# First loads on two queues, roots by GpSimd pow, and a first unit halved along its contraction

## The chip, the cores and the metric

The kernel runs on one core of one Trainium2 chip. The metric is the device time in microseconds (us) of one execution. Engine names are those of the profile: PE is TensorE, DVE is VectorE, ACT is ScalarE, POOL is GpSimd, SP is SyncE. PEld is PE's weight load; a q after a name (SPq) is that engine's sequencer, which issues the loads. In the profile's names xn is normalized x, tp its transpose as PE writes it, sp_ps the output of the warm-up, and bp a product of the Fourier part, which ACT copies to Bs.

## The reference, cut to what matters

```python
def _layernorm(x, axis=-1, eps=1e-5):
    m = jnp.mean(x, axis=axis, keepdims=True); v = jnp.var(x, axis=axis, keepdims=True)
    return (x - m) / jnp.sqrt(v + eps)

def reference(A_x, A_w_r, A_w_i, B_x, B_w_gate, B_w_up, B_w_down):
    # _A_ref: irfft2(rfft2(xn) * (w_r + 1j * w_i)), over 2048 x 512
    # _B_ref: (gelu(xn @ w_gate) * (xn @ w_up)) @ w_down, 512 -> 1792 -> 512
    x = A_x                                   # 1 x 2048 x 512, bf16
    xn = _layernorm(x, axis=-1)
    return x + _A_ref(xn, A_w_r, A_w_i) + _B_ref(xn, B_w_gate, B_w_up, B_w_down)
```

## The kernel before

The rows of x are cut into 16 chunks of 128 rows. Chunks 0 and 1 are loaded singly, normalized, transposed on PE and multiplied at once with the first 512 columns of the gate weights (Wg) and up weights (Wu). PE can do nothing useful before that, so the kernel has it multiply zeros ("spin"), first on zeros alone, then on x chunk 0 (x0), to get its clock up. A small planner in the kernel orders all later work from hand-written estimates of durations and landing times; that order is fixed when the kernel is built.

```python
    pin(nc.scalar.activation(out=root[:], in_=eps_t[:], func=AF.Sqrt, ...))   # loads the Sqrt table
    load_x(0, 1); load_x(1, 1)                       # all on nc.sync
    nc.sync.dma_start(out=idx_t[:], ...)             # a small index table
    load_w(Wg_sb, 0, 512); load_w(Wu_sb, 0, 512)
    load_x(2, 2)
    # ... further loads of weights and x, all on nc.sync
    for k in range(25):                              # warm-up of PE
        pin(nc.tensor.matmul(sp_ps[:, :P if k < 20 else D], lhsT=spin[:],
                             rhs=spin[:] if k < 20 else x_t[:, 0, :], start=True, stop=True))
    def spin_on():                                   # six more, after x0's transposes
        for k in range(6):
            nc.tensor.matmul(sp_ps[:, :256], lhsT=spin[:], rhs=x_t[:, 0, :256], ...)
    # ...
    # 1/sqrt(var + eps): chunks 0, 1 by ACT's Sqrt and DVE's reciprocal;
    # chunks 2, 3 by a bit trick and two Newton steps on DVE (8 instructions),
    # chunks 4 to 15, four at a time, the same way on POOL (10 instructions, then 2 for a bias)
```

## Time and profile before

| | before |
|---|---|
| median time (3 runs; 4 with the rounds of the changed kernel) | 179.47 us (179.32) |
| span of the profiled run | 177.5 us |
| PE busy | 172.1 us, 97% |
| x0 lands, first statistics start | 3.00 us |
| first g_ps (gate product of the first unit) | 6.34 us |
| first u_ps (up product of the first unit) | 7.79 us |
| first y_ps (down phase) | 119.52 us |

The first view is the page's busy table and the chain of work that ended last, as shares of the span, of the kernel before.

```profile
PE 172.1 (97%) x1115; PEld 96.0 (54%) x1133; DVE 116.6 (66%) x261; ACT 96.5 (54%) x171; POOL 20.1 (11%) x60
...
PE 83%; ACT 5%; DMA 3%; issue 3%; POOL 2%; DVE 1%; SPq 1%; ACTq 0%
```

PE is the limit. After the first u_ps it has next to no idle time, so a gain must come from the first 8 us, or from one of the few gaps left. PE's waits name one such gap, 0.4 us. The columns are the waiting instruction, what it waited for, the total, the count and the longest.

```profile
PE bp L581 <- ACT Bs L551: 0.4, 1, 0.4
```

The next view is the timeline of the kernel before: start, duration, engine, line, operation, output and inputs, shape, count; in brackets the idle time before it and what ended that.

```profile
0.80 0.86 SPq L271 DMA_DIRECT2D x_t<-in_A_x_dram  x2
...
2.18 0.43 SPq L275 DMA_DIRECT2D Wg_sb<-in_B_w_gate_dram  x1
2.65 0.51 SPq L275 DMA_DIRECT2D Wu_sb<-in_B_w_up_dram  x1
3.00 0.69 DVE L338 BATCH_NORM_STATS2 stats<-x_t 128x6 f32<-128x512 bf16 x1 [1.99 <-DMA x_t<-in_A_x_dram]
```

The same kernel's PE alone:

```profile
1.05 2.31 PE L318 MATMUL sp_ps<-spin 128*128 128x128 bf16 x20 [1.05 <-DVE eps_t L264]
3.16 2.34 PE L318 MATMUL sp_ps<-x_t,spin 128*128 128x512 bf16 x5
5.29 0.56 PE L350 MATMUL tp<-ident_t,xn 128*128 128x128 bf16 x4
5.69 0.82 PE L323 MATMUL sp_ps<-x_t,spin 128*128 128x256 bf16 x6
6.34 0.61 PE L505 MATMUL g_ps<-xnT,Wg_sb 128*128 128x128 bf16 x8
...
7.04 0.61 PE L505 MATMUL g_ps<-xnT,Wg_sb 128*128 128x128 bf16 x8
7.79 1.07 PE L505 MATMUL u_ps<-xnT,Wu_sb 128*128 128x128 bf16 x16
```

PE starts at 1.05 us and, up to the transposes (tp), never stops. The merged durations overlap, so the pace is to be read from starts. The 20 warm-up matmuls of 128 columns take from 1.05 to 3.16: 106 ns each. The six of 256 columns take from 5.69 to 6.34, again 108 ns each, for twice the columns. Between the two PE's clock doubled. "Half clock" below means the pace of about 107 ns for 128 columns, "full clock" the pace of about 55.

### The profile page before, as it was taken

The numbers are of one execution on the slowest core, as the hardware profiler recorded it, in microseconds if no ns is written. First come the engines' busy times: TensorE is split into PE (matmuls) and PEld (weight loads), VectorE is DVE, ScalarE is ACT, GpSimd is POOL, SyncE is SP. The second block draws the span as 40 slices with busy tenths as digits, with TensorE's granted clock in tenths as the row PEclk, the third lists the DMA queues.
The fourth block names the chain that finished last, engine by engine and source line by source line (L and its number), as shares of the span: only waits on it lengthen the run. The fifth ranks groups of instructions, "written<-read, shape, count | busy, mean of one in ns | idle before, by whom it ended". The sixth has DMA issues, their size and how long they took to land.

```text
span 177.5 us, 3118 instructions
## 1 busy us (share of the span) xinstructions
PE 172.1 (97%) x1115; PEld 96.0 (54%) x1133; DVE 116.6 (66%) x261; ACT 96.5 (54%) x171; POOL 20.1 (11%) x60
## 2 busy tenths in 40 slices
PE   7999999998999999999999999999999999999993
PEld 5798845464455554555555545454445444444463
DVE  3499999873933599998699999543526334344333
ACT  4463286979575989799999955453112111211200
POOL 1000534810676000000000000000000000000000
DMA  3999994243282752121202520200132222221212
GB/s 92 350 382 378 368 180 92 59 98 55 60 291 95 245 173 59 33 55 31 63 6 55 148 60 5 59 0 4 51 97 89 72 78 63 89 85 62 78 44 59
DMA packets 21872, 19.36 MB, mean 109 GB/s; under 512 B 8480, under 2 KB 20000, under 8 KB 21856
## 3 DMA queue, kind: packets, MB, share of 16 engines
q1 hardware_dynamic: 21440, 17.84, 34.6%
q0 software_dynamic: 416, 1.32, 2.5%
q8 instruction: 9, 0.15, 0.3%
q14 instruction: 7, 0.06, 0.1%
HBM read 13.38 MB, written 2.10 MB: 87 GB/s over the span
## 4 chain that ended last, share of the span: by engine, by line
PE 83%; ACT 5%; DMA 3%; issue 3%; POOL 2%; DVE 1%; SPq 1%; ACTq 0%
PE y_ps L820 27%; PE u_ps L505 23%; PE g_ps L505 22%; DMA Wu_sb<-in_B_w_up_dram 3%; PE dp L639 2%; ACT Bs L551 2%; PE yp L772 2%; PE gp L742 2%; PE y_ps L824 2%; PE ep L648 2%; ACT xn L467 2%; ACT ge L510 1%; DVE hT L515 1%; PE bp L581 1%; POOL t L366 0%
## 5 line engine op out<-in xcount | busy, mean ns | idle before, releaser
L505 PE MATMUL u_ps<-xnT,Wu_sb 128*128 128x512 bf16 (+2 forms) x267 | 56.9, 341 | 0.3
L505 PE MATMUL g_ps<-xnT,Wg_sb 128*128 128x512 bf16 (+2 forms) x265 | 56.4, 340 | 0.4
L515 DVE TENSOR_TENSOR hT<-u_ps,ge 128x512 bf16<-128x512 f32 x56 | 38.5, 688 | 19.0 <-PE u_ps L505 10.5
L820 PE MATMUL y_ps<-Wd_sb,hT 128*128 128x512 bf16 (+2 forms) x246 | 50.6, 355 | 0.3
L510 ACT ACTIVATE ge<-g_ps 128x512 bf16<-128x512 f32 x56 | 33.9, 606 | 21.4 <-PE g_ps L505 17.6
L505 PEld LDWEIGHTS <-Wu_sb 128*128 128x128 bf16 x272 | 24.9, 98 | 21.4 <-DMA Wu_sb<-in_B_w_up_dram 0.3
L505 PEld LDWEIGHTS <-Wg_sb 128*128 128x128 bf16 x272 | 24.8, 98 | 20.0
L820 PEld LDWEIGHTS <-hT 128*128 128x128 bf16 x252 | 23.2, 98 | 22.4
L778 ACT CAST yf<-yp 128x512 bf16<-128x512 f32 x16 | 9.3, 586 | 40.5 <-PE yp L772 40.5
L827 DVE TENSOR_TENSOR y_sb<-y_ps,y_sb 128x512 bf16<-128x512 f32 (+2 forms) x18 | 11.1, 631 | 30.0 <-PE y_ps L824 30.0
L653 ACT CAST E<-ep 64x512 bf16<-64x512 f32 x32 | 18.6, 580 | 1.3 <-PE ep L648 0.8
L338 DVE BATCH_NORM_STATS2 stats<-x_t 128x6 f32<-128x512 bf16 x16 | 10.5, 677 | 3.9 <-DMA x_t<-in_A_x_dram 3.9
L467 ACT ACTIVATE xn<-x_t,nb,rstd 128x512 bf16<-128x512 bf16 x12 | 9.7, 827 | 1.8 <-POOL nb L378 1.8
L551 ACT CAST Gs<-gp 128x512 bf16<-128x512 f32 x16 | 8.9, 592 | 0.9 <-PE gp L742 0.9
L551 ACT CAST ds<-dp 128x512 bf16<-128x512 f32 x16 | 9.0, 597 | 0.6 <-PE dp L639 0.5
L551 ACT CAST Bs<-bp 128x512 bf16<-128x512 f32 x16 | 8.4, 607 | 0.5 <-PE bp L581 0.5
L784 DVE TENSOR_TENSOR lv<-yf 128x512 bf16<-128x512 bf16 x16 | 6.1, 422 | 1.5 <-ACT yf L778 0.6
L772 PEld LDWEIGHTS <-Gs 128*128 128x128 bf16 x64 | 4.8, 98 | 3.5
L791 DVE TENSOR_TENSOR yt<-lv 128x512 bf16<-128x512 bf16 x16 | 6.1, 422 | 0.3
L824 PE MATMUL y_ps<-yt,RI_t 128*128 128x512 bf16 (+2 forms) x18 | 6.1, 355 | 0.0
L772 PE MATMUL yp<-CT,Gs 128*128 128x128 bf16 x64 | 6.0, 219 | 0.0
L742 PEld LDWEIGHTS <-F 128*128 128x128 bf16 x64 | 4.5, 98 | 2.6
(72 smaller groups left out, 123.2 us busy)
## 6 DMA issues: line engine op xcount, KB each, us to landing
F<-F SPq DMA_DIRECT2D x32, 64.0 KB, 2.0
y_sb<-in_A_x_dram SPq DMA_DIRECT2D x16, 128.0 KB, 2.1
out_dram<-y_sb SPq DMA_DIRECT2D x15, 128.0 KB, 1.7
x_t<-in_A_x_dram SPq DMA_DIRECT2D x7, 256.0 KB, 8.6
Wd_sb<-in_B_w_down_dram SPq DMA_DIRECT2D x1, 1792.0 KB, 7.5
Wg_sb<-in_B_w_gate_dram SPq DMA_DIRECT2D x2, 512.0 KB, 5.2
Wu_sb<-in_B_w_up_dram SPq DMA_DIRECT2D x2, 512.0 KB, 7.4
Wg_sb<-in_B_w_gate_dram SPq DMA_DIRECT2D x1, 768.0 KB, 10.4
```

The costliest lines, as they stand in the source:

```text
L338: V.bn_stats(out=st[:], in_=x_t[:, c, :])
L467: xn_op[c] = add("ACT", 0.72, lambda c=c: A.activation(out=xn[:, c, :], in_=x_t[:, c, :], func=AF.Identity, bias=nb[:, c:c + 1], scale=rst ...
L505: T_.matmul(b[name][:, f], lhsT=W_[:, e, (f0 + f) * P:(f0 + f + 1) * P], rhs=rhs[:, e, :], start=(e == 0), stop=(e == NE - 1))
L510: A.activation(out=b["ge"][:], in_=b["g_ps"][:], func=AF.Gelu_apprx_tanh)
L515: V.tensor_tensor(out=hT_of(sb, f0, m, o, w), in0=b["u_ps"][:], in1=b["ge"][:], op=ALU.mult)
L551: A.copy(out=o, in_=i)
L653: A.copy(out=b["E"][64 * h:64 * h + 64, r], in_=b["ep", h][64 * r:64 * r + 64])
L772: T_.matmul(t[:, q], lhsT=late["G"][:, q, c0 + j], rhs=IQ[q], start=(q == 0), stop=(q == 3), skip_group_check=True)
L778: A.copy(out=b["yf"][:, j], in_=b[j][:])
L820: T_.matmul(b[o][:], lhsT=hT_of(sb, f, 1, cl * P, P)[:, 0], rhs=Wd_sb[:, f, o:o + w], start=(f == 0), stop=False)
L824: T_.matmul(b[o][:], lhsT=late["RI"][:, c, :], rhs=late["yt"][:, c, o:o + w], start=False, stop=True)
L827: V.tensor_tensor(out=b["y"][:, o:o + w], in0=b[o][:], in1=b["y"][:, o:o + w], op=ALU.add)
```

## The change

Its intent is to start the real matmuls sooner. The first four loads are issued by two sequencers at once. The warm-up on x0 becomes shorter, so that it does not stand before the transposes. The first unit's gate product starts on the first half of the contraction. Roots after the first two chunks take two GpSimd instructions instead of eight on DVE or ten on GpSimd. The planner's figures of landing times are moved to match, and with them the order of later instructions.

```diff
-    pin(nc.scalar.activation(out=root[:], in_=eps_t[:], func=AF.Sqrt, ...))
-    load_x(0, 1)
-    load_x(1, 1)
+    pin(load_x(0, 1))
+    pin(load_x(1, 1, nc.scalar))
+    pin(load_w(Wg_sb, 0, 512))
+    pin(load_w(Wu_sb, 0, 512, nc.scalar))
+    pin(nc.scalar.activation(out=warm[:], in_=eps_t[:], func=AF.Sqrt, ...))
-    nc.sync.dma_start(out=idx_t[:], ...)      # now issued after the loads of x
-    load_w(Wg_sb, 0, 512)
-    load_w(Wu_sb, 0, 512)
     ...
-    for k in range(25):
-        pin(nc.tensor.matmul(sp_ps[:, :P if k < 20 else D], lhsT=spin[:],
-                             rhs=spin[:] if k < 20 else x_t[:, 0, :], ...))
+    for k in range(32):
+        pin(nc.tensor.matmul(sp_ps[:, :P], lhsT=spin[:],
+                             rhs=spin[:] if k < 20 else x_t[:, 0, :P], ...))
     def spin_on():
         for k in range(6):
-            nc.tensor.matmul(sp_ps[:, :256], lhsT=spin[:], rhs=x_t[:, 0, :256], ...)
+            nc.tensor.matmul(sp_ps[:, :P], lhsT=spin[:], rhs=x_t[:, 0, :P], ...)
     ...
-    def rsqrt_steps(U, c0, n): ...             # bit trick and two Newton steps
+    def root_eps(c0, n):                       # y = var + eps; y = pow(y, -0.5)
+        plus_eps(nc.gpsimd, c0, n)
+        nc.gpsimd.tensor_tensor(out=y, in0=y, in1=minus_half[:, 0:n], op=ALU.pow)
     ...
-        g = split("g_ps", "G", Wg_sb, 1000 + k, WG_LAND, 2 if k == 0 else m)
+        if k == 0:                             # e = 0, 1 after the first copy, e = 2, 3 after the second
+            g = add("PE", occ / 2, lambda: mm_half(0), [xT_op[0, 0]], ...)
+            g = add("PE", occ / 2, lambda: mm_half(1), [xT_op[0], g], ...)
     # cut: planner's landing times, chunk 1's copy moved to DVE, the last phase's first group in four pieces
```

## The prediction

> **What bounds the kernel.** TensorE. The busy table has it busy 172.1 of 177.5 us; the chain that ended last is 83% PE. From the first real matmul (g_ps, 6.34 us in the timeline) to the last (174.7) PE hardly stops: the table by stretches leaves about 1.5 us idle, of which the waits name 0.31 us for the second weight tile (Wu lands at 7.74) and 0.45 us at 40.9 (bp, for ACT's copies). So the change can mainly win by starting the real stream earlier. The tail, 2.8 us after the last matmul, is untouched.
>
> **The head now (timeline).** x_t is there at 3.0; statistics 0.69, mean, sqrt on ACT, reciprocal; xn's first half at 4.58, second to 5.26. The first transposes begin at 4.98, the rest only at 5.29, behind five warm-up matmuls of 512 columns (3.16 to about 5.3). Copies end at 6.24. SyncE issues everything: Wg at 2.18 (lands about 6.3), Wu at 2.65 (7.74). After g_ps and four transposes u_ps starts at 7.79; no gap until 40.9.
>
> **What changes.**
> - Wg is issued about 0.95 us and Wu 1.4 us sooner. The Trainium skill, "DMA: Bandwidth & Descriptors", section "Issuing engines are not separate DMA queues", says both issuers run on the same 16 engines and only issue time is saved; the trace fits (Wg, Wu, x2-3 arrive as one stream, 512 KB in 1.44 us, 365 GB/s). I estimate Wg at 5.5 to 6.2 (it now shares with Wu), Wu at 6.5 to 6.9, x2-3 at 7.5 to 8.1.
> - Shorter warm-up lets the transposes start when xn is there, and the first unit starts on half the contraction: g_ps at 5.7 to 6.1. After 16 matmuls (0.94 us) and four transposes (0.23), u_ps at about 6.8: 0.9 to 1.0 us gained.
> - Chunks 2-3: eight DVE steps (1.55 us, 9.98 to 11.53) become two GpSimd steps. Its small steps come every 0.28 us; I take pow for one of these, so 0.6 us with hand-overs. But PE now reaches these transposes at about 10.3 instead of 12.66 (fewer matmuls in front), and VectorE puts one hT product (0.69) before xn. I expect a new PE wait of 0.2 to 0.5 us.
> - Later fours: ten GpSimd steps before the bias become two, 2.2 us less each time, but PE does not wait for that chain: little, perhaps part of the 0.45 us.
> - Last phase's first group cut in four, Wd before RI: nothing.
>
> **On the critical path:** +0.95 (head) -0.3 (chunks 2-3) +0.2 (bp): about 0.9 us.
>
> **Predicted: 178.6 us, range 177.7 to 179.5.** Faster by over 2%: 0.02; within 2%: 0.96; slower: 0.02.
>
> **What would show it.** First g_ps at 5.7 to 6.1, first u_ps near 6.8 with hardly a wait for Wu; first statistics still at 3.0 to 3.2; pow 0.2 to 0.3 us; a PE gap of 0.2 to 0.5 near 10.5 before the transposes; from 45 us on everything about 0.9 us earlier, the down phase at about 118.2 instead of 119.1, at the same pace; same tail.
>
> **What would make it wrong.** (1) The clock: the skill's "TensorE: Matmul & The Clock Gate", Part 1, says PE runs at half rate until a window of some 3.4 us was busy. This trace: 107 to 115 ns per 128 columns until about 5.6, 55 after. The shorter warm-up leaves PE idle between about 4.5 and 5.0; if the full clock comes later, up to 32 matmuls cost 50 ns more each, and the gain is gone. (2) pow slow on GpSimd; over 1 us it stalls PE directly. (3) Wg landing at 6.5, sharing with Wu. (4) x0 sharing with x1, coming later and pushing the whole head.

## The result, and the profile after

The changed kernel takes 180.24 us (median of 4, 180.05 to 180.50), the kernel before 179.32 (median of 4). Executions over 1.5% slower than the fastest of the same kernel are left out of the means. Ratios here are the mean time of one kernel's runs over that of the other's of the same rounds, so they are not quite the ratio of the quoted medians. This one is 1.0054, with a 95% interval of 1.0033 to 1.0074. The change costs 0.9 us; a gain of 0.7 was forecast.

The busy table and the chain of the changed kernel:

```profile
PE 173.5 (97%) x1140; PEld 97.4 (55%) x1140; DVE 116.0 (65%) x255; ACT 95.6 (54%) x170; POOL 17.3 (10%) x38
...
PE 95%; DMA 2%; DVE 1%; issue 0%
```

PE is a little busier, for the same real work (of the 25 further records seven are warm-up, and 18 are matmuls whose records the trace before lacks). Most of that extra time is the half clock, which the timeline shows. Here are the lines that answer to those of before. The ACTq line of x1 is new; Wu is issued by ACTq at 1.23.

```profile
0.80 0.40 ACTq L273 DMA_DIRECT2D x_t<-in_A_x_dram  x1
...
0.80 0.39 SPq L273 DMA_DIRECT2D x_t<-in_A_x_dram  x1
...
1.23 0.46 ACTq L277 DMA_DIRECT2D Wu_sb<-in_B_w_up_dram  x1
1.25 0.42 SPq L277 DMA_DIRECT2D Wg_sb<-in_B_w_gate_dram  x1
...
3.99 0.69 DVE L340 BATCH_NORM_STATS2 stats<-x_t 128x6 f32<-128x512 bf16 x1 [2.97 <-DMA x_t<-in_A_x_dram]
```

PE alone, changed kernel, up to 9.5 us (the last line is cut there; u_ps has 16 matmuls):

```profile
1.05 2.31 PE L320 MATMUL sp_ps<-spin 128*128 128x128 bf16 x20 [1.05 <-DVE minus_half L266]
4.00 1.44 PE L320 MATMUL sp_ps<-x_t,spin 128*128 128x128 bf16 x12 [0.64 <-DMA x_t<-in_A_x_dram]
5.98 0.71 PE L352 MATMUL tp<-ident_t,xn 128*128 128x128 bf16 x4 [0.53 <-DVE xn L346]
6.49 0.85 PE L325 MATMUL sp_ps<-x_t,spin 128*128 128x128 bf16 x6
7.13 1.91 PE L499 MATMUL g_ps<-xnT,Wg_sb 128*128 128x128 bf16 x16
8.83 0.56 PE L352 MATMUL tp<-ident_t,xn 128*128 128x128 bf16 x4
9.23 0.44 PE L491 MATMUL u_ps<-xnT,Wu_sb 128*128 128x128 bf16 x5
```

First, x0's statistics start at 3.99 instead of 3.00, although x0 is still the first load of its queue and is issued at the same 0.80. Second, the 16 gate matmuls take from 7.13 to 8.83, 106 ns each: PE is at half clock all through the first unit's gate product and the transposes after it, until about 9.2. The first u_ps comes 1.44 us later than before. The down phase starts at 120.58 instead of 119.52, 1.06 later, so 0.38 us is won back in between; the wait of bp for ACT is no longer in PE's list. The tail of 2.8 us after the last matmul is unchanged.

The landing times, from the table of DMA issues (KB each, median us from issue to landing), before and then after:

```profile
x_t<-in_A_x_dram SPq DMA_DIRECT2D x2, 128.0 KB, 2.3
```

```profile
Wu_sb<-in_B_w_up_dram ACTq DMA_DIRECT2D x1, 512.0 KB, 6.2
...
x_t<-in_A_x_dram ACTq DMA_DIRECT2D x1, 128.0 KB, 3.4
x_t<-in_A_x_dram SPq DMA_DIRECT2D x1, 128.0 KB, 3.2
```

The two single chunks of x took 2.3 us; now they take 3.2 and 3.4. Wu, issued at 1.23, lands at about 7.4 (1.23 + 6.2) instead of 7.74, so issuing it 1.4 us sooner brought 0.3.

### The profile page after: what moved, and what is told of

The parts are those of the page before. It is cut to its first block, busy times and chain, and to the rows that moved or that the text cites. A ratio compares the mean times of both kernels' runs of the same rounds, so it can differ in the third digit from the quotient of the medians.

```text
span 178.5 us, 3122 instructions
## 1 busy us (share of the span) xinstructions
PE 173.5 (97%) x1140; PEld 97.4 (55%) x1140; DVE 116.0 (65%) x255; ACT 95.6 (54%) x170; POOL 17.3 (10%) x38
## 4 chain that ended last, share of the span: by engine, by line
PE 95%; DMA 2%; DVE 1%; issue 0%
PE u_ps L491 27%; PE y_ps L818 27%; PE g_ps L491 27%; PE gp L739 2%; PE yp L769 2%; PE dp L636 2%; PE bp L578 2%; PE y_ps L822 2%; PE ep L645 2%; DMA x_t<-in_A_x_dram 2%; PE tp L352 1%; PE g_ps L499 1%; DVE stats L340 1%; PE sp_ps L325 0%; DVE xn L346 0%; DVE y_sb L825 0%
## 5 line engine op out<-in xcount | busy, mean ns | idle before, releaser
L491 PEld LDWEIGHTS <-Wg_sb 128*128 128x128 bf16 x256 | 23.9, 98 | 20.6
L453 ACT ACTIVATE xn<-x_t,nb,rstd 128x512 bf16<-128x512 bf16 x12 | 9.2, 803 | 1.5 <-POOL nb L371 1.5
L645 PE MATMUL ep<-ds,CT 128*128 128x512 bf16 x16 | 5.7, 379 | 0.0
```

What stands on the lines that cost most here:

```text
L491: T_.matmul(b[name][:, f], lhsT=W_[:, e, (f0 + f) * P:(f0 + f + 1) * P], rhs=rhs[:, e, :], start=(e == 0), stop=(e == NE - 1))
L645: T_.matmul(t[:], lhsT=cc("L" if g + h else "L0"), rhs=b["ds", h][:], start=True, stop=True)
```

## The experiments

There are two suspects. Theory S: the second queue makes x0 late, and the head follows x0. Theory C: the shorter warm-up leaves gaps on PE, and the clock comes up late. Edits are against the changed kernel unless said otherwise. Every result was correct. The experiments ran in four sets of four, each on another chip and beside its own runs of the kernel before; the medians of before in the four sets were 179.27, 179.37, 179.51 and 179.47. A profile is of one execution, and executions differ in when the clock comes up, so a profile and the median can show different cases; where they do, it is said. The medians in the table are those of all runs of a kernel in these sets; between kernels of different sets the ratios are the better comparison. No kernel differs from the one before by 2 percent; what is read below is whether an interval leaves 1 out.

| run | what differs | median us (lowest to highest) | ratio to before (95%) |
|---|---|---|---|
| changed kernel | | 180.24 (180.05 to 180.50) | 1.0054 (1.0033 to 1.0074) |
| loads_back | loads as before | 178.95 (178.80 to 180.15) | 0.9981 (0.9968 to 0.9995) |
| loads_only | before, with the new loads | 180.28 (179.49 to 181.24) | 1.0051 (1.0021 to 1.0081) |
| x1_scalar | only x1 on ACT | 180.35 (180.07 to 180.56) | 1.0058 (1.0045 to 1.0070) |
| wu_scalar | only Wu on ACT | 180.98 (179.54 to 182.08) | 1.0080 (1.0052 to 1.0107) |
| all_sync | x0, x1, Wg, Wu on SP | 179.42 (178.76 to 180.03) | 0.9991 (0.9969 to 1.0014) |
| wg_behind_x0 | x0, Wg, x1, Wu on SP | 181.25 (180.89 to 181.31) | 1.0103 (1.0088 to 1.0118) |
| after_warm | longer warm-up only | 178.98 (178.81 to 179.59) | 0.9983 (0.9967 to 0.9999) |
| sync_warm | loads_back, longer warm-up | 179.24 (178.85 to 179.55) | 0.9994 (0.9979 to 1.0009) |
| fill_first | only the first gap closed | 179.01 (178.89 to 179.60) | 0.9976 (0.9958 to 0.9993) |
| fill_last | only the second gap closed | 179.16 (178.74 to 180.60) | 0.9990 (0.9961 to 1.0019) |
| short_warm_only | before, with the short warm-up | 179.60 (179.14 to 180.80) | 1.0015 (0.9983 to 1.0046) |
| x1_quiet | after_warm, x1 alone on ACT, Wg late | 179.91 (179.82 to 179.93) | 1.0016 (0.9997 to 1.0036) |
| pow_only | before, with pow | 178.86 (178.65 to 179.07) | 0.9960 (0.9944 to 0.9975) |
| no_half | after_warm, first unit whole | 179.50 (179.37 to 179.85) | 0.9999 (0.9985 to 1.0013) |
| all_sync_warm | all_sync, longer warm-up | 178.83 (178.50 to 179.17) | 0.9961 (0.9943 to 0.9979) |
| best_root | all_sync_warm, planner told pow's time | 178.26 (178.02 to 178.55) | 0.9935 (0.9920 to 0.9950) |

### The loads back, and the loads alone

loads_back:

```diff
-    pin(load_x(1, 1, nc.scalar)); pin(load_w(Wg_sb, 0, 512)); pin(load_w(Wu_sb, 0, 512, nc.scalar))
+    load_x(1, 1); nc.sync.dma_start(out=idx_t[:], ...); load_w(Wg_sb, 0, 512); load_w(Wu_sb, 0, 512)
```

> The changed kernel with the loads as before (all four on SyncE, index table third); everything else of the change stays. Theory S (x0's landing at 3.97 instead of 3.0 us comes from the second queue's transfers on the same engines, and the head follows x0): first statistics back at 3.0, u_ps first at 7.8 or earlier, about 179.0 to 179.4 us in all. Rival C (most of the loss is the tensor clock, because the shorter warm-up leaves gaps): the first 16 g_ps matmuls still take about 107 ns each though x0 is on time, first u_ps at 8.2 or later, 179.8 to 180.2 us.

Measured: 178.80 to 179.08 in five of six executions, and 180.15 in the profiled one. In the profiled one x0 was on time (statistics at 3.05), and still g_ps ran at half clock (first g_ps 6.76, transposes 8.44). So neither theory fits alone: with x0 on time the kernel is mostly fast, but the half clock can come anyway.

loads_only puts the change's load block, diffed above, into the kernel before and leaves the rest of that kernel alone.

> The kernel before with only the change's four loads on alternating queues (index table late); warm-up, roots and first unit as before. Theory S: x0's statistics start at 3.9 to 4.0 us, the head moves by about 0.9 us, the whole is 0.6 to 1.0 us slower than before (180.0 to 180.4). Rival C: the long warm-up keeps the clock up, so at most 0.3 us slower (179.3 to 179.7).

Measured: statistics at 4.03 and first u_ps at 8.87 (7.79 before), so the late x0 comes with the loads alone. The long warm-up held the clock in the profiled execution: g_ps and u_ps ran at 55 ns. Theory S is right about x0.

### What makes x0 late

x1_scalar and wu_scalar each put one of the two loads back on SP:

```diff
 x1_scalar:
-    pin(load_w(Wu_sb, 0, 512, nc.scalar))
+    pin(load_w(Wu_sb, 0, 512))
 wu_scalar:
-    pin(load_x(1, 1, nc.scalar))
+    pin(load_x(1, 1))
```

> The changed kernel with Wu back on SyncE, behind Wg; x1 alone on ScalarE's queue. If x0 is late by fair sharing of bytes with whatever the other queue holds, x0 now shares only with x1's 128 KB: statistics at 3.2 to 3.5 us. If any second queue delays the completion, at 3.9 as in the changed kernel. If only Wu's many packets matter, at 3.0 to 3.1. Total between 179.0 (head in time, clock up) and 180.2.

> The changed kernel with x1 back on SyncE behind x0; Wu alone on ScalarE's queue, issued at 0.8 us beside x0. Fair sharing of bytes: Wu's 512 KB compete with x0 from the first byte and x1 waits behind x0: statistics of x0 at 3.9 to 4.3 us, x1 later still, 180.2 to 181. If only the order of issue mattered (x0 is first on its own queue either way), 3.0 to 3.2.

Measured: statistics of x0 at 4.08 in x1_scalar and 4.07 in wu_scalar, in both as late as with both loads moved. Fair sharing of bytes does not fit: x1 brings 128 KB and Wu 512 KB, and the delay is the same. In wu_scalar x1, which waits behind x0 on the same queue, was late as well (its statistics start at 5.89), and the run is slower still.

all_sync and wg_behind_x0 have no second queue at all:

```diff
 all_sync:        SP: x0, x1, Wg, Wu
-    pin(load_x(1, 1, nc.scalar)); pin(load_w(Wg_sb, 0, 512)); pin(load_w(Wu_sb, 0, 512, nc.scalar))
+    pin(load_x(1, 1)); pin(load_w(Wg_sb, 0, 512)); pin(load_w(Wu_sb, 0, 512))
 wg_behind_x0:    SP: x0, Wg, x1, Wu
+    pin(load_w(Wg_sb, 0, 512)); pin(load_x(1, 1)); pin(load_w(Wu_sb, 0, 512))
```

> The changed kernel with all four loads on SyncE's queue in the order x0, x1, Wg, Wu, index table late. Theory S2 (any transfer on a second queue in the first microseconds delays x0's completion by about 1 us): no second queue, so statistics of x0 at 3.0 to 3.1 us, Wg landing about 0.4 us before its 6.3 in the kernel before, u_ps at 7.0 to 7.4 where the clock is up; 178.3 to 178.9 us. Rival W (x0 is delayed by a big weight load that begins before x0 has finished, whatever its queue): Wg is issued at 1.7 here instead of 2.2, statistics at 3.3 to 4.0, 179 to 180.

> All on SyncE's queue, but in the order x0, Wg, x1, Wu, so that Wg is issued at 1.2 us right behind x0 as in the changed kernel. Theory S2: x0's statistics still at 3.0 to 3.1 (x1 later, 5 to 6 us, behind Wg). Rival W: x0 at 3.8 to 4.1 as in the changed kernel.

The first DVE work of wg_behind_x0 (timeline):

```profile
3.00 0.69 DVE L340 BATCH_NORM_STATS2 stats<-x_t 128x6 f32<-128x512 bf16 x1 [1.98 <-DMA x_t<-in_A_x_dram]
...
5.66 0.69 DVE L340 BATCH_NORM_STATS2 stats<-x_t 128x6 f32<-128x512 bf16 x1 [1.75 <-DMA x_t<-in_A_x_dram]
```

x0 is on time at 3.00 with Wg right behind it on the same queue, issued at 1.24 as in the changed kernel. So a weight load behind x0 is not enough; it takes the second queue. x1, now behind Wg's 512 KB, starts its statistics at 5.66, and that makes this order slow: PE waits 2.21 us for xn, and g_ps then runs at half clock (8.00 to 9.67). In all_sync x0 was somewhat late in the profiled execution (3.45), and 3.18 and 3.10 in the two later kernels with the same loads (all_sync_warm, best_root). The times of all_sync split: three at 178.76 to 179.01, three at 179.82 to 180.03. The profiled one is of the second kind, with a gap of 0.53 us before the transposes and g_ps at half clock; only two of the six lie in the 178.3 to 178.9 expected with the clock up.

x1_quiet asks whether the second queue is enough by itself. It starts from after_warm (below):

```diff
     pin(load_x(0, 1)); pin(load_x(1, 1, nc.scalar))
+    pin(nc.sync.dma_start(out=idx_t[:], in_=rows_d)); pin(nc.sync.dma_start(out=idx2[:], in_=rows_d))
     pin(load_w(Wg_sb, 0, 512))
-    pin(load_w(Wu_sb, 0, 512, nc.scalar))
+    pin(load_w(Wu_sb, 0, 512))
```

> The kernel of after_warm, but only x1 on ScalarE's queue, and two small index loads on SyncE before Wg, so that Wg is issued at about 2.2 us as in the kernel before and nothing but x0 and x1 move until then. Theory S2 (a transfer of a second queue at the same time delays x0's completion by 1 us): statistics at 3.9 to 4.1. Rival (x0 needs both a second queue and a weight load behind it): 3.0 to 3.3.

```profile
3.68 0.69 DVE L343 BATCH_NORM_STATS2 stats<-x_t 128x6 f32<-128x512 bf16 x1 [2.67 <-DMA x_t<-in_A_x_dram]
```

Neither expectation held: 3.68. About two thirds of the delay is there with x1 alone on the second queue and Wg issued no sooner than in the kernel before (2.17). The rest seems to come when weights follow sooner; with one profile each, the share is rough.

That the second queue makes x0 late is firmer: in the nine profiled kernels with one queue the statistics start at 3.00 to 3.45, in the nine with two at 3.68 to 4.24. A rival goes with the second queue in all nine: ACT's own issues push its table load from 0.79 to between 1.22 and 1.72. The packed traces speak against it as traffic: in none of the 18 does a packet of a queue other than those of the loads start between 0 and 5 us. They also show the form of the delay. Each load gives 16 completion marks, and the statistics start after the last. In the kernel before x0's come at 2.62 to 2.97; in the changed kernel 14 come at 2.97 to 3.21 and the last two at 3.89 and 3.96. The size and form of the delay are measured; its mechanism is not. The Trainium skill, "DMA: Bandwidth & Descriptors", section "Queues, rings and completion order", says that a load's completion mark lands only after every earlier write of the same DMA engine, across its queues. A second queue's writes could then hold up x0's marks on some of the engines. That would fit, but no run here shows it.

### The clock

after_warm leaves the loads alone and makes the warm-up long enough for PE to be busy until the transposes:

```diff
-    for k in range(32):   # 20 on zeros, 12 on x0
+    for k in range(46):   # 28 on zeros, 18 on x0
```

> The changed kernel with the warm-up made long enough to fill PE until the transposes (28 without data, 18 on x0, instead of 20 and 12); x0 still late at 3.97. Theory: about 0.8 us of the loss is the half clock under g_ps's first 16 matmuls, which the gaps at 3.36 to 4.00 and 5.3 to 5.98 caused: 179.2 to 179.6 us, g_ps matmuls 55 ns each. Rival (the clock depends on the window's phase and not on the gaps; the loss is x0's delay only): stays at 180.0 to 180.4, g_ps still at 107 ns.

This is the run that decides. The first view is the summary of the g_ps line in the changed kernel (duration in ns, lowest, median, highest), the second the same in after_warm:

```profile
L499 PE MATMUL g_ps<-xnT,Wg_sb x16: 311/311/311, 7.1 to 8.7; 128*128 128x128 bf16 x16
```

```profile
L499 PE MATMUL g_ps<-xnT,Wg_sb x16: 219/219/219, 6.7 to 7.5; 128*128 128x128 bf16 x16
```

PE's timeline of after_warm:

```profile
1.05 3.17 PE L320 MATMUL sp_ps<-spin 128*128 128x128 bf16 x28 [1.05 <-DVE minus_half L266]
4.01 2.13 PE L320 MATMUL sp_ps<-x_t,spin 128*128 128x128 bf16 x18
5.93 0.59 PE L352 MATMUL tp<-ident_t,xn 128*128 128x128 bf16 x4
6.36 0.50 PE L325 MATMUL sp_ps<-x_t,spin 128*128 128x128 bf16 x6
6.69 1.06 PE L499 MATMUL g_ps<-xnT,Wg_sb 128*128 128x128 bf16 x16
7.58 0.39 PE L352 MATMUL tp<-ident_t,xn 128*128 128x128 bf16 x4
7.81 1.06 PE L491 MATMUL u_ps<-xnT,Wu_sb 128*128 128x128 bf16 x16
```

x0 is still late (warm-up on x0 from 4.01), but g_ps takes 0.89 us instead of 1.70, and u_ps starts at 7.81 instead of 9.23. The time falls by 1.26 us, from 180.24 to 178.98 (medians of different sets; the ratios to before are 1.0054 and 0.9983), which is more than was expected. Of the 1.42 us at u_ps, the parts read from the two timelines are 0.81 (g_ps), 0.31 (the six matmuls before it: 6.49 to 7.13 against 6.36 to 6.69), 0.25 (the eight transposes of chunks 0 and 1: 0.51 and 0.40 against 0.43 and 0.23), and 0.05 from x0. The half clock alone is more than the whole loss.

It also shows that the late x0 and the head's savings cancel: with the clock up, u_ps starts at 7.81 against 7.79 before.

Which gap keeps the clock down? The changed kernel has two: 0.64 us before x0 (3.36 to 4.00) and about 0.5 us between warm-up and transposes. fill_first has 28 on zeros and 12 on x0, fill_last 20 and 18:

```diff
 fill_first:
-    for k in range(32):   # 20 on zeros, 12 on x0
+    for k in range(40):   # 28 on zeros, 12 on x0
 fill_last:
+    for k in range(38):   # 20 on zeros, 18 on x0
```

> The changed kernel with 28 instead of 20 warm-up matmuls without data; the 12 on x0 as they are. Closes PE's gap of 0.64 us before x0 arrives; the gap of 0.5 us before the transposes stays. If the wait for the late x0 is what keeps the clock down: 178.9 to 179.3 us, as after_warm. If the second gap is: 180.0 to 180.5, as the changed kernel. If only the sum counts: mixed, some near 179 and some near 180.2.

> The changed kernel with 18 instead of 12 warm-up matmuls on x0; the gap before x0 stays, the gap before the transposes is closed. If the wait for the late x0 keeps the clock down: 180.0 to 180.5. If the second gap does: 178.9 to 179.3. If only the sum counts: mixed.

Measured: fill_first 178.89 to 179.60, none slow; its profiled execution, the slowest, has the full clock at g_ps (219 ns) and waits 0.7 us for Wu. fill_last: four at 178.74 to 179.20 and two at 180.54 and 180.60, the profiled one of them with g_ps at 314 ns. With both gaps open all four executions of the changed kernel were slow, and all six of x1_scalar (180.07 to 180.56). So closing either gap helps; none in six against two in six is too few to say that the wait for the late x0 matters more. Nor is a gap before the transposes harmless: with x0 on time or nearly so it goes with the half clock in the profiled executions of loads_back (0.40 us) and all_sync (0.53 us). In fill_first it comes after 4.5 us of unbroken work, and the transposes that follow it are already at full clock.

The kept traces can be counted for this. The moment at which the clock rose, read from the durations of single matmuls, lies between 3.9 and 7.0 us in 11 of the 18 profiled executions and between 9.1 and 12.2 in the other seven. Of the ten in which PE stood still for 0.35 us or more before the transposes, seven are late; of the eight others, none. So a gap makes the late rise likely and does not force it. This is the link between the two suspects: the second queue delays x0, the delay opens a gap on PE, and the gap makes it likely that the clock stays down.

sync_warm is loads_back with 17 instead of 12 matmuls on x0 (`range(37)`, the first 20 on zeros):

> The kernel of loads_back with 17 instead of 12 warm-up matmuls on x0, so that PE has no gap from 1.05 us to the first transposes. Theory C (the clock rises only when a whole window was busy; the gap of 0.4 us before the transposes lets some executions start g_ps at half clock, as loads_back's profiled execution at 180.15 against 178.8 to 179.1 of its others): no execution over 179.2, g_ps at about 55 ns each in the profile, 178.7 to 179.0. If the window's phase alone decides: again one or two in six near 180.

Measured: 178.85 to 179.55. The slow case near 180.2 is gone in six executions, but the bound I set, 179.2, was exceeded by three. In the profiled one PE had no gap up to the transposes and still the clock rose only within g_ps (durations 219 to 314 ns). So a warm-up without gaps does not fix the moment; it makes a very late one rarer.

short_warm_only is the kernel before with the change's two warm-up hunks (diffed above) and nothing else:

> The kernel before with only the change's warm-up (12 matmuls of 128 columns on x0 instead of 5 of 512, 6 of 128 instead of 6 of 256 after the first transposes); loads, roots and first unit as before. Theory C: PE is idle from 4.5 to 5.0 us, so some executions reach g_ps at half clock and take 0.8 to 1.2 us more: at least two of six at 179.9 to 180.5, the others at 179.0 to 179.3. Rival (the loss needs x0 late as well): all six within 179.0 to 179.5.

Measured: 179.14 to 180.80, two of six above 180.5. The scatter agrees with theory C, but the profiled execution (179.73) does not show its cause: it had the full clock at g_ps, and waited 0.9 us for Wg, which landed 0.6 us later than in the kernel before. This run is inconclusive on its own.

### The roots by pow

pow_only is the kernel before with pow in all later roots:

```diff
-        m = [add("DVE", 1.5, lambda: [f() for f in steps], m, key=-1190)]
+        m = [add("POOL", 0.5, lambda: root_eps(2, 2), m, key=-1190, lat=0.6)]
     # and for each later four:
+        m = [add("POOL", 0.5, lambda: root_eps(c0, 4), m, key=c0, lat=0.6)]
+        m = [add("POOL", 0.7, lambda: bias(c0, 4), m, key=c0 + 1, lat=0.9)]
```

> The kernel before with only the roots by GpSimd pow (chunks 2-3 and the later fours). pow took 0.73 us in the changed kernel instead of the 0.28 I had assumed, so xn of chunk 2 is ready about 0.2 us before its time in the kernel before; PE's order now has the transposes earlier. Theory: a PE wait of 0 to 0.3 us near 11.4, and the 0.45 us wait of bp near 41 gone: 178.8 to 179.3. Rival (the slow pow costs the change its gain): 179.6 or more.

Measured: 178.86, ratio 0.9960. This part of the change is a gain of 0.4 percent by itself. The changed kernel's summary of the pow line shows what it costs (the shortest is the one of 128 x 2, the others 128 x 4):

```profile
L362 POOL TENSOR_TENSOR rstd<-rstd,minus_half x4: 726/1032/1037, 11.7 to 33.9; 128x4 f32<-128x4 f32 x3, 128x2 f32<-128x2 f32 x1
```

0.73 us for two elements per partition and 1.03 for four, where the plain product of two such operands (128 x 4) took 0.20 in the first four and 0.71 in the two later ones. I had assumed 0.28. It is still faster than the Newton steps: in the kernel before a later four took GpSimd from 19.05 to 22.40, 3.35 us; in the changed kernel from 20.99 to 22.97, 1.98. PE's waits in pow_only:

```profile
PE tp L352 <- DVE xn L346: 0.3, 1, 0.3
PE u_ps L493 <- DMA Wu_sb<-in_B_w_up_dram: 0.2, 1, 0.2
```

The wait of bp for ACT is gone. The 0.3 us for xn is not pow's: it lies before chunk 0's transposes at 5.05, because in this execution the clock rose during the warm-up, which so ended early. pow's own wait, not in the list, is about 0.23 us: eight matmuls from 10.49 end at 11.36 at the usual pace, and chunk 2's transposes start at 11.59. From the first u_ps to the first y_ps PE takes 111.36 us in pow_only (7.80 to 119.16), 111.35 in the changed kernel and 111.73 in the kernel before. So pow, with the reordering that the planner makes of it, can account for all of the 0.38 us that the changed kernel wins back after the head.

### The halved first unit

no_half is after_warm with the first unit's gate product in one piece:

```diff
-        if k == 0:
-            g = add("PE", occ / 2, lambda: mm_half(0), [xT_op[0, 0]], ...)
-            g = add("PE", occ / 2, lambda: mm_half(1), [xT_op[0], g], ...)
-        else:
-            g = split("g_ps", "G", Wg_sb, 1000 + k, WG_LAND, m)
+        g = split("g_ps", "G", Wg_sb, 1000 + k, WG_LAND, m)
```

> The kernel of after_warm with the first unit's gate product in one piece again (waits for both copies, not the first). Theory: in after_warm g_ps starts at 6.69 us while the second copy ends at 6.89, so the halving is worth at most 0.2 us: g_ps at 6.9 to 7.0, 178.9 to 179.2 us, not separable from after_warm's 178.98. Rival (the halving carries the head's gain): 0.4 us or more slower, 179.4 and up.

Measured: 179.50, 0.5 us over after_warm by the medians and 0.3 by the ratios to before, whose intervals overlap (0.9985 to 1.0013 against 0.9967 to 0.9999). It lies where the rival was expected, but its profile does not put that on the halving. g_ps starts at 6.64 (6.69 in after_warm); PE then waits 0.6 us for Wu, and a wait of bp for ACT of 0.3 us is back, probably because the planner ordered later work differently. fill_first, with the halving, waits 0.7 us for Wu in the same way. What the halving is worth by itself stays open.

### A version that beats both

all_sync_warm joins the loads of all_sync with 24 warm-up matmuls on zeros and 15 on x0:

```diff
-    pin(load_x(1, 1, nc.scalar)); pin(load_w(Wg_sb, 0, 512)); pin(load_w(Wu_sb, 0, 512, nc.scalar))
+    pin(load_x(1, 1)); pin(load_w(Wg_sb, 0, 512)); pin(load_w(Wu_sb, 0, 512))
-    for k in range(32):   # 20 on zeros, 12 on x0
+    for k in range(39):   # 24 on zeros, 15 on x0
```

> Candidate for the best: all_sync (four loads on SyncE, index table late) with PE kept busy until the transposes (24 warm-up matmuls without data, 15 on x0). Theory: x0 at 3.0 to 3.5 us, the full clock from about 5.7, so g_ps at 55 ns, Wg and Wu 0.4 us sooner than before: u_ps first at 7.2 to 7.5 against 7.79; 178.4 to 178.9 us and none of six over 179.3. Rival (clock depends on phase alone): mixed as all_sync, 178.8 to 180.

Measured: 178.83, none over 179.17, where three of six of all_sync were over 179.8: with the same loads, closing PE's gap takes the slow kind away. u_ps starts at 7.53. One loss is left: the eight matmuls before the transposes of chunks 2 and 3 start at 10.22 and take 0.87 us at the usual pace, but the transposes start at 11.35, so PE waits 0.26 us for pow.

best_root tells the planner that a root takes 1.1 us, and it then puts 16 instead of 8 matmuls before those transposes:

```diff
-    ROOT = 0.5
+    ROOT = 1.1
```

> Candidate for the best: all_sync_warm with the planner told 1.1 instead of 0.5 us for a root, so that it puts 16 instead of 8 matmuls of 256 columns before the transposes of chunks 2-3. Theory: PE's wait of 0.26 us at 11.1 goes, 178.4 to 178.8 us (all_sync_warm 178.83). Rival: nothing gained because the next weight tile or the copies become the wait: 178.7 to 179.1.

```profile
5.18 0.67 PE L352 MATMUL tp<-ident_t,xn 128*128 128x128 bf16 x4
...
6.06 1.06 PE L499 MATMUL g_ps<-xnT,Wg_sb 128*128 128x128 bf16 x16
...
7.25 1.07 PE L491 MATMUL u_ps<-xnT,Wu_sb 128*128 128x128 bf16 x16
```

Measured: 178.26, ratio 0.9935, 1.2 us under the kernel before and a little better than expected. Its u_ps starts at 7.25, and no wait of PE after the warm-up's start is left in the list.

## Why the prediction was wrong

- **What bounds the kernel, and where the gain must come from: right.** PE bounds it; the change acted in the first 9 us and at one gap near 41.
- **x0 on time ("first statistics still at 3.0 to 3.2"): wrong**, 3.99. I had read the skill's section "Issuing engines are not separate DMA queues" (page "DMA: Bandwidth & Descriptors") as: nothing lost, issue time saved. The runs agree that little is gained, but with a second queue x0 was late by 0.7 to 1.2 us (3.68 to 4.24 against 3.00). I had named this as risk 4 and put nothing into the sum for it.
- **Wg at 5.5 to 6.2, Wu at 6.5 to 6.9: wrong.** Wg landed at about 6.35 (1.25 + 5.1, the shortest of its three) and Wu at about 7.4. Issued 0.95 and 1.4 us sooner, they landed 0.05 later and 0.3 sooner.
- **The head's gain of 0.95: the step that failed.** u_ps came 1.44 us later instead of 1.0 sooner. after_warm splits that: 1.37 us is the half clock, and the late x0 eats nearly all of what the shorter path gives. The half clock was risk 1, in the right form ("up to 32 matmuls cost 50 ns more each"), but as a risk and not in the sum. A gap of 0.5 us was in the forecast; the gap of 0.64 us before it, which the late x0 opened, was not; with it closed (fill_first) none of six executions was slow. The number of matmuls was about right: 16 of g_ps, six before them and eight transposes ran slowly, 30 in all. The skill, "TensorE: Matmul & The Clock Gate", Part 1, says that the full clock needs a busy window of some 3.4 us, and that the window is free-running. The runs agree in kind: PE was busy 2.31 us, then idle, and the clock stayed down until about 9.2.
- **A new PE wait of 0.2 to 0.5 us before chunks 2 and 3: right in kind**, about 0.13 before the first transpose in the changed kernel (8 matmuls from 11.91 end at 12.78, transposes at 12.91) and 0.26 in all_sync_warm, where PE is earlier. The figure for pow was wrong (0.28 against 0.73).
- **Later fours: 2.2 us less each: wrong size**, 1.37 in the first four, because pow on four elements takes 1.03. The consequence drawn ("perhaps part of the 0.45") was right in kind and too small: 0.38 instead of 0.2.
- **Tail and the down phase's pace: right.**

In sum: forecast +0.95 - 0.3 + 0.2 gained, measured about -1.44 (head) + 0.38 (pow and order) in the profile, which makes about -1.06 at the first y_ps, and 0.9 us slower in the medians.

## What to carry to other kernels

Treat the warm-up of PE as part of the critical path: shortening it to let real work in sooner saved here only where no gap opened before PE was at full pace, and a gap opens as soon as the first load slips. Issuing early loads from a second sequencer is no free gain when the first load is what everything waits for: here one queue, with only the small table load taken out from between the first loads, did better (all_sync 0.9991, changed kernel 1.0054). When a planner orders the instructions, measure a new instruction's duration and give it to the planner; here the two kernels that differ in that one number were 0.57 us apart (178.83 and 178.26, in different sets; 0.47 by the ratios; 0.28 us of it is already there at the first u_ps of the profiled executions, where the number plays no part).

## What the Trainium skill lacked or had wrong

- "TensorE: Matmul & The Clock Gate", Part 1, puts the transition at about 4 us of activity, within 500 ns. Here it moved more: in the 11 profiles with an early rise it came 2.9 to 5.9 us after PE's first matmul. pow_only and the kernel before have the same warm-up; its five matmuls of 512 columns took 1.62 us in pow_only (so the clock rose among them, at about 3.9 us) and 2.34 before (all at half clock, to about 5.3). In sync_warm, with no gap from 1.05 us to the transposes, the first g_ps at 6.30 was still at half clock.
- The same page does not say how much idle time within a window keeps the clock down. Here gaps of 0.64 and about 0.5 us together went with it in four of four executions; the second gap alone, after longer unbroken work (fill_first), in none of six; and a single gap of 0.40 us (loads_back) in at least the profiled one of six.
- The same page, "Seeing it yourself", warns that clock events in a trace can be unreliable, and sets the pace of the matmuls beside them. It does not say that the profile's granted clock can miss the half clock altogether: the granted clock of the changed kernel's profile reads 1.00 in the stretch from 6.31 to 7.79 us, where 128 columns took 106 ns. The pace of the matmuls was the safer reading here.
- "DMA: Bandwidth & Descriptors", section "Issuing engines are not separate DMA queues", says what a second issuer saves and not what it can cost: the landing of the first 128 KB went from 2.2 to 3.2 us after issue.
- "GPSIMD Engine Reference" has no figure for pow: 0.73 us for 128 x 2 and 1.03 for 128 x 4, against 0.20 (at its shortest) for a product of 128 x 4.
